# Attention, then two matmul layers, on one core: first loads also from ScalarE's queue, the 1e-9 of the sums on GpSimd, and a new order

## The chip, the cores and the metric

The kernel runs on one core of a Trainium2 chip. The core has five engines that run side by side, each with its own in-order queue of instructions: PE (TensorE, matmuls and transposes), DVE (VectorE), ACT (ScalarE), POOL (GpSimd) and SP (SyncE, which here only issues DMAs). The metric is the device time of one execution in microseconds (us). Three timed runs of the kernel before gave 943.40, 943.42 and 945.23 us; their median is 943.42 us.

## The reference

```
q, k, v: (4 batches, 8 heads, 576 positions, 64)
scores = q @ k.T / 8 + bias            # bias = -slope[head] * distance
scores = where(0 <= row - col < 128, scores, -1e9)
attn = exp(scores - rowmax);  attn = attn / (rowsum(attn) + 1e-9)
x = (attn @ v) laid out as (4*576, 512)
h = x @ w_in                            # 512 -> 2048
g = (a0 + a1 h + a2 h^2 + a3 h^3) / (1 + |b0| |h| + |b1| h^2 + 1e-6)
x = g @ w_out                           # 2048 -> 512
out = (relu(x @ w2_in) ** 2) @ w2_out
```

The weights are 64-bit floats in memory. The kernel makes two fp32r numbers, a high and a low part, of each, and each large matmul is done three times (high by high, high by low, low by high).

## The kernel before, in words

**Attention.** Two heads of one batch are a pair; there are 16 pairs (p0 to p15). Each has five row tiles (units): four of 128 rows and one of the last 64. For a pair, PE transposes q and k (`tr`, L340, and `trr`, L349, for the last 64 rows, which are loaded for all heads of a batch at once into `rem` and `remv`, L316), DVE or ACT copies them from PSUM to `qkT` (L291 or L289), PE makes the scores (`s`, L380 and L369), DVE adds the bias and takes the row extreme (`e`, `st`, L391), ACT takes exp and the row sums (`e`, `sums`, L407), PE transposes the result (`pt`, L442, L437), DVE or ACT copies it (`ptsb`), and PE multiplies it by v (`o`, L468; `or`, L477, L481). The sums of a pair, 9 columns wide, get 1e-9 added (L414) and are inverted (L415), both on DVE, into `rc`. PE transposes `rc` (L420), it is copied to `rt` and sent to memory (`rs`), as is the unnormalised output (`xT` to `xs`).

**Weights.** In the gaps of the attention, the 64 chunks of the weights are loaded (`win1r`, `wout1r`, ...) and split: `w_exp` (L206 on ACT, L209 on POOL or DVE), three steps on DVE (L214, L216, L218), the rounding to the high part (L222, L226) and the subtraction for the low part (L229).

**The two layers.** Blocks of 512 tokens. For the first layer `xs` and `rs` are loaded again (`xr`, and `R`, which spreads one row over 64 partitions, L666), multiplied (L674), and split into `xh` (L226 or L222) and `xl` (L229). The input of the first block comes from batch 0, so the split of its four column groups (c = 0 to 3, from pairs 0 to 3) is done while the attention of later pairs runs. The matmuls are `h` (L694) and `y` (L778).

**What sets the order.** The class `Plan` lists all operations with their engines, costs and predecessors, and orders them one at a time by earliest possible start; ties are broken by a priority in which a table, `BIAS`, adds a number for each kind of operation. The chosen order is then written out: every engine's queue holds its instructions in that order, and an engine whose next instruction waits does nothing else. `warm` (L613) are 22 matmuls on an identity matrix at the start, with no result that is used. All loads are issued by SP before; each DMA uses one of eight completion semaphores in turn, so a DMA waits, at its issue, for the one that stood eight places ahead.

## Time and profile before

| | us |
|---|---|
| median of three runs | 943.42 |
| the profiled execution | 942.65 |
| its span | 940.9 |
| PE busy in the span | 923.6 |
| DVE, ACT, POOL busy | 625.9, 494.9, 324.0 |

The profile is of one execution. Its own time is 1.75 us above its span, and 0.77 us below the median. In the views, busy time is the time in which an engine had at least one instruction running; "idle before" is the engine's idle time just ahead of an instruction, and the arrow names what ended it. "SPq" is a DMA issue by SP.

### The profile page before, as it was taken

The page shows a single profiled execution, that of the slowest core. Times are in us where ns is not written, and L with a number is a line of the kernel's source. Part 1 is how long each engine was busy: PE and PEld are TensorE (multiplying, and loading weights), DVE is VectorE, ACT ScalarE, POOL GpSimd, SP SyncE. Part 2 cuts the span into 40 slices and gives each one's busy share as a digit, 9 for nine tenths or more (in the row PEclk, how much of TensorE's full clock was granted, in tenths as well). Part 3 has the DMA queues.
Part 4 walks back from the last instruction along what each step waited for, and adds up shares of the span by engine and source line. Part 5 has one row for each costly group of instructions (what it writes and reads, how often), then busy time and mean ns, then how long its engine had stood idle before and what let it go on. Part 6 is the DMA issues. An engine that isn't in the chain of part 4 may idle for free.

```text
span 940.9 us, 14096 instructions
## 1 busy us (share of the span) xinstructions
PE 923.6 (98%) x4908; PEld 759.5 (81%) x4908; DVE 625.9 (67%) x1285; ACT 494.9 (53%) x1072; POOL 324.0 (34%) x343
## 2 busy tenths in 40 slices
PE   7999999999999999999999999999999999999998
PEld 5666667888998888888888888888888888888897
DVE  3999998999888886887799987862233223222232
ACT  4988887767767555655666654432222222222222
POOL 5354236867455446444666731030010001000000
PEclk9999999999999999999999999999999999999999
DMA  8999963322402100400142254302000200100010
GB/s 183 236 227 242 241 190 120 115 91 67 132 27 78 35 1 1 125 10 1 37 143 90 68 179 160 133 23 89 1 1 16 74 0 1 68 1 1 1 45 22
DMA packets 102311, 77.01 MB, mean 82 GB/s; under 512 B 64465, under 2 KB 89441, under 8 KB 102241
## 3 DMA queue, kind: packets, MB, share of 16 engines
q1 hardware_dynamic: 102240, 76.12, 28.7%
q8 instruction: 38, 0.62, 0.3%
q14 instruction: 33, 0.26, 0.1%
HBM read 61.87 MB, written 14.23 MB: 81 GB/s over the span
## 4 chain that ended last, share of the span: by engine, by line
PE 87%; DVE 8%; ACT 3%; DMA 1%; issue 1%; SPq 0%; POOL 0%; POOLq 0%; DVEq 0%; ACTq 0%
PE y L778 42%; PE h L694 40%; DVE e L391 3%; ACT e L407 2%; PE tr L340 1%; PE pt L442 1%; DVE wb L218 1%; PE warm L613 1%; DVE qkT L291 1%; DVE wb L216 1%; DMA win1r<-in_moe_w_in_dram 1%; DMA wout1r<-in_moe_w_out_dram 1%; PE o L468 0%; DVE ptsb L291 0%; DVE win1r L214 0%
## 5 line engine op out<-in xcount | busy, mean ns | idle before, releaser
L222 ACT ACTIVATE gh<-h 128x512 fp32r<-128x512 f32 (+1 forms) x160 | 88.7, 555 | 182.4 <-PE y L778 153.4
L229 DVE TENSOR_TENSOR gl<-h,gh 128x512 fp32r<-128x512 f32 (+1 forms) x160 | 101.7, 636 | 122.3 <-ACT gh L222 121.7
L755 DVE SCALAR_TENSOR_TENSOR h<-h,ah 128x512 f32<-128x512 f32 (+1 forms) x80 | 51.6, 645 | 115.0 <-ACT ah L751 114.8
L694 PE MATMUL h<-xh,win1hi 128*128 128x512 f32 (+1 forms) x320 | 118.1, 369 | 1.0 <-DVE gl L229 1.0
L694 PE MATMUL h<-xl,win1hi 128*128 128x512 f32 (+1 forms) x320 | 117.8, 368 | 0.0
L778 PE MATMUL y<-gh,wout1hi 128*128 128x512 f32 (+1 forms) x320 | 117.8, 368 | 0.0
L778 PE MATMUL y<-gl,wout1hi 128*128 128x512 f32 (+1 forms) x320 | 117.7, 368 | 0.0
L694 PE MATMUL h<-xh,win1lo 128*128 128x512 f32 (+1 forms) x320 | 117.7, 368 | 0.0
L778 PE MATMUL y<-gh,wout1lo 128*128 128x512 f32 (+1 forms) x320 | 117.7, 368 | 0.0
L694 PE MATMUL h<-xh,win2lo 128*128 128x512 f32 (+1 forms) x320 | 117.7, 368 | 0.0
L694 PE MATMUL h<-xl,win2hi 128*128 128x512 f32 (+1 forms) x320 | 117.7, 368 | 0.0
L694 PE MATMUL h<-xh,win2hi 128*128 128x512 f32 (+1 forms) x320 | 117.6, 368 | 0.0
L778 PE MATMUL y<-wout2hi,gh 128*128 128x512 f32 x288 | 112.2, 390 | 0.0
L778 PE MATMUL y<-wout2hi,gl 128*128 128x512 f32 x288 | 112.2, 390 | 0.0
L778 PE MATMUL y<-wout2lo,gh 128*128 128x512 f32 x288 | 112.1, 389 | 0.0
L751 ACT ACTIVATE ah<-h 128x512 f32<-128x512 f32 (+1 forms) x80 | 44.4, 554 | 120.9 <-PE h L694 120.4
L719 POOL TENSOR_SCALAR t<-ah,ab_sb 128x512 f32<-128x512 f32 (+1 forms) x80 | 61.7, 772 | 130.6 <-ACT ah L707 114.4
L721 POOL TENSOR_TENSOR t<-t,ah 128x512 f32<-128x512 f32 (+1 forms) x80 | 99.3, 1241 | 5.5
L226 POOL TENSOR_SCALAR xh<-xr 128x512 fp32r<-128x512 f32 (+1 forms) x20 | 13.2, 664 | 249.9 <-PE h L694 248.7
L407 ACT ACTIVATE e<-e,st 128x256 f32<-128x256 f32 (+1 forms) x144 | 67.0, 467 | 8.9 <-DVE st L391 8.7
L694 PEld LDWEIGHTS h<-xh,win1hi 128*128 128x128 f32 x320 | 60.4, 189 | 11.3 <-DVE gl L229 1.3
L694 PEld LDWEIGHTS h<-xh,win2hi 128*128 128x128 f32 x320 | 60.3, 189 | 10.6
(121 smaller groups left out, 1878.7 us busy)
## 6 DMA issues: line engine op xcount, KB each, us to landing
win1r<-in_moe_w_in_dram SPq DMA_DIRECT2D x16, 512.0 KB, 4.8
wout1r<-in_moe_w_out_dram SPq DMA_DIRECT2D x16, 512.0 KB, 3.5
win2r<-in_moe_w_in_dram SPq DMA_DIRECT2D x16, 512.0 KB, 3.8
wout2r<-in_moe_w_out_dram SPq DMA_DIRECT2D x16, 512.0 KB, 3.5
xs<-xT SPq DMA_DIRECT2D x16, 288.0 KB, 4.7
out_dram<-yt SPq DMA_DIRECT2D x18, 256.0 KB, 2.3
vr<-in_v_dram SPq DMA_DIRECT2D x32, 128.0 KB, 3.8
ys<-yt SPq DMA_DIRECT2D x16, 256.0 KB, 2.3
```

What stands on the lines that cost most here:

```text
L216: nc.vector.scalar_tensor_tensor(wb, wb, 3, lw, ALU.logical_shift_left, ALU.bitwise_or)
L222: nc.scalar.activation(dst, src, AF.Copy)
L226: nc.gpsimd.tensor_scalar(dst, src, 1.0, 1.0, ALU.mult, ALU.mult)
L229: (nc.vector if eng == "DVE" else nc.gpsimd).tensor_tensor(dst, a, b, ALU.subtract)
L391: nc.vector.tensor_tensor_reduce(d["e"][:, j, :w], d["s"] if last else d["s"][j], biasl[hp // 2][:, hp % 2, :w] if last else bias8[hp][:, ...
L407: nc.scalar.activation(e, e, AF.Exp, scale=-1.0, bias=s[:, j : j + 1], accum_out=sums[p % 3][:, c : c + 1],)
L694: nc.tensor.matmul(h[:, :n], a[:, c * P : (c + 1) * P], bb[:, :n], start=(m == 0), stop=(m == 3 * NCC - 1),)
L719: nc.gpsimd.tensor_scalar(gt("t", 2, ji, f), ah, ab_sb[:, 1:2], ab_sb[:, 0:1], ALU.mult, ALU.add)
L721: nc.gpsimd.tensor_tensor(tl["t", ji, f], tl["t", ji, f], ah, ALU.mult)
L751: nc.scalar.activation(gt("ah", 2, ji, f), tl["h", ji, f], AF.Relu)
L755: nc.vector.scalar_tensor_tensor(h, h, 0.0, tl["ah", ji, f], ALU.max, ALU.mult)
L778: nc.tensor.matmul(dst, a, bb, start=(f == 0 and m == 0), stop=(f == NF - 1 and m == 2))
```

## The change

Three things. The loads of the first two pairs (`load_qk`, `load_v`, `load_rem`) may be issued by ACT as well as by SP, at the planner's choice. The addition of 1e-9 (`plus`) moves from DVE to POOL, ahead of the reciprocal, which stays on DVE; the exp that writes over the sums three pairs later now waits for `plus` and no longer for the reciprocal. And the table `BIAS` has new numbers, which together with the planner's new entries give a new order on every engine.

```diff
-            if eng == "SP":
+            if self.ops[name][4]:
                 free["DMA"] = max(free.get("DMA", 0.0), end + self.QUEUE) + self.ops[name][4]
...
-BIAS = {'W0': -416.9, 'W1': -833.9, 'W2': 174.9, ...
+BIAS = {'W0': -327.0, 'W1': -452.1, 'W2': 534.2, ...
...
+    def queue(eng):
+        return nc.scalar if eng == "ACT" else nc.sync
...
-            nc.sync.dma_start(
+            queue(eng).dma_start(
                 t[:, t0:t1, j, :], src[b, h0 + j, t0 * P : t1 * P, :].rearrange("(t p) d -> p t d", p=P)
...
+    def plus(p):
+        t = st[p]["rc"] = ap2.tile([P, NSUM], F32, tag="rc", name=f"rc{p}")
+        nc.gpsimd.tensor_scalar(t, sums[p % 3], 1e-9, 1.0, ALU.add, ALU.mult)
+
     def rcp(p):
-        t = st[p]["rc"] = ap2.tile([P, NSUM], F32, tag="rc", name=f"rc{p}")
-        nc.vector.tensor_scalar(t, sums[p % 3], 1e-9, None, ALU.add)
-        nc.vector.reciprocal(t, t)
+        nc.vector.reciprocal(st[p]["rc"], st[p]["rc"])
...
+    def two(p, cost=1.15):
+        return {"SP": cost, "ACT": cost} if p < 2 else {"SP": cost}
...
-                    after=[("ttr", u, j), ("rcp", p - 3)], prio=u,
+                    after=[("ttr", u, j), ("plus", p - 3)], prio=u,
...
-            ("rcp", p), lambda p=p: rcp(p), DVE=0.16,
-            after=[("exp", u, j) for u in range(u0, u0 + NQ) for j in range(2)] + [("rtp", p - 2)], prio=u0 + 4.2, port=True,
-        )
+            ("plus", p), lambda p=p: plus(p), Pool=0.12,
+            after=[("exp", u, j) for u in range(u0, u0 + NQ) for j in range(2)] + [("rtp", p - 2)], prio=u0 + 4.2,
+        )
+        plan.add(("rcp", p), lambda p=p: rcp(p), DVE=0.2, after=[("plus", p)], prio=u0 + 4.2)
```

The new order at three places. The first is the start, on ACT, up to the first exp (`e0`). The number behind a tile's name is its pair (or unit, for `e` and `pt`); the last number only counts buffers. DMAHW0 to DMAHW7 are the eight completion semaphores. Before:

```order
L160 ACT_TABLE_LOAD
L289 ACTIVATE qkT0_214<-tr0_0_0_211 128x256 [waits PE_49]
L289 ACTIVATE qkT0_214<-tr1_0_0_221 128x256 [waits PE_49]
L289 ACTIVATE qkT0_214<-tr0_0_2_231 128x256 [waits PE_49]
L289 ACTIVATE qkT0_214<-tr1_0_2_238 128x256 [waits PE_49]
L407 ACTIVATE e0_259,sums0_154<-e0_259,st0_258 128x128 [waits DVE_49]
```

And now, on the same engine, up to the same exp:

```order
L160 ACT_TABLE_LOAD
L311 DMA qr0_167<-in_q_dram 128x2x64 x2
L311 DMA kr0_164<-in_k_dram 128x2x64
L311 DMA kr0_164<-in_k_dram 128x2x64 [waits DMAHW0_49]
L289 ACTIVATE qkT0_204<-tr0_0_0_201 128x256 [waits PE_49]
L289 ACTIVATE qkT0_204<-tr1_0_0_213 128x256 [waits PE_49]
L319 DMA rem_0_229<-in_q_dram 64x8x64 [waits DMAHW3_49]
L319 DMA rem_0_229<-in_k_dram 64x8x64 [waits DMAHW4_49]
L319 DMA remv0_150<-in_v_dram 64x8x64 [waits DMAHW7_49]
L410 ACTIVATE e0_262,sums0_154<-e0_262,st0_261 128x128 [waits DVE_49]
```

Four loads of pair 0 now stand right behind the table load, two of the four copies have gone to DVE, and the three loads of the last 64 rows of batch 0 stand ahead of the first exp. SP issues kr0, vr0, the second half of qr0, vr1, qr1, win1r of chunk 0 and kr1 in this time; the semaphore that remv0 waits for, DMAHW7, is the one that the first load of kr1 uses just before.

On PE the start reads so before:

```order
L613 MATMUL warm_167<-ident_107 128x128 x16
L340 MATMUL tr0_0_0_211<-ident_107,qr0_182 128x128 x2
L613 MATMUL warm_167<-ident_107 128x128 x3
L340 MATMUL tr1_0_0_221<-ident_107,kr0_162 128x128 x2
L613 MATMUL warm_167<-ident_107 128x128 x3
L340 MATMUL tr0_0_2_231<-ident_107,qr0_182 128x128 x2
L340 MATMUL tr1_0_2_238<-ident_107,kr0_162 128x128 x2
L380 MATMUL s0_0_0_246<-qkT0_214 128x128
```

And now:

```order
L623 MATMUL warm_170<-ident_107 128x128 x11
L343 MATMUL tr0_0_0_201<-ident_107,qr0_167 128x128 x2
L623 MATMUL warm_170<-ident_107 128x128 x2
L343 MATMUL tr1_0_0_213<-ident_107,kr0_164 128x128 x2
L623 MATMUL warm_170<-ident_107 128x128 x9
L343 MATMUL tr0_0_2_233<-ident_107,qr0_167 128x128 x2
L343 MATMUL tr1_0_2_242<-ident_107,kr0_164 128x128 x2
L383 MATMUL s0_0_0_246<-qkT0_204 128x128
```

The first transposes stand five `warm` matmuls earlier; the number of `warm` matmuls ahead of the first scores is 22 as before.

The second place is POOL around the input of the first layer's column group 1 (`xr0_1`). Before:

```order
L209 TENSOR_SCALAR wb6_870<-win1r_6_746 128x512
L229 TENSOR_TENSOR win1lo_6_928<-wb6_870,win1hi_6_927 128x512
L674 TENSOR_TENSOR xr0_1_820<-xr0_1_820,R0_1_822 128x512
L226 TENSOR_SCALAR xh0_1_992<-xr0_1_820 128x512
L229 TENSOR_TENSOR xl0_1_1004<-xr0_1_820,xh0_1_992 128x512
L229 TENSOR_TENSOR win1lo_7_1056<-wb7_969,win1hi_7_1055 128x512
```

And now:

```order
L209 TENSOR_SCALAR wb5_827<-win1r_5_681 128x512
L684 TENSOR_TENSOR xr0_1_737<-xr0_1_737,R0_1_739 128x512
L226 TENSOR_SCALAR xh0_1_868<-xr0_1_737 128x512
L229 TENSOR_TENSOR xl0_1_886<-xr0_1_737,xh0_1_868 128x512
L417 TENSOR_SCALAR rc4_913<-sums1_155 128x9
L226 TENSOR_SCALAR win1hi_5_916<-wb5_827 128x512
```

The addition of 1e-9 for pair 4 stands behind the three operations on column group 1; that of pair 3 stands in the same way behind group 0, and that of pair 5 behind group 2.

The third place is PE at the change from attention to the first layer. Before:

```order
L442 MATMUL pt77_2342<-ident_107,e77_2298 128x128 x4
L369 MATMUL s15_2_2351<-qkT15_2202 64x192 x2
L468 MATMUL o15_2360<-ptsb15_2326,vr15_2138 64x256 x4
L442 MATMUL pt78_2373<-ident_107,e78_2304 128x128 x4
L437 MATMUL pt79_2381<-ident_107,e79_2366 128x128 x2
L694 MATMUL h0_0_2388<-xh0_0_804,win1hi_0_317 128x512
...
L468 MATMUL o15_2360<-ptsb15_2326,vr15_2138 64x256 x2
L420 MATMUL or15_2502<-ident_107,rc15_2384 9x128
```

And now:

```order
L372 MATMUL s15_2_2358<-qkT15_2223 64x192 x2
L447 MATMUL pt77_2366<-ident_107,e77_2315 128x128 x4
L473 MATMUL o15_2382<-ptsb15_2356,vr15_2156 64x256 x4
L704 MATMUL h0_0_2390<-xh0_0_719,win1hi_0_348 128x512
...
L425 MATMUL or15_2497<-ident_107,rc15_2388 9x128
L447 MATMUL pt78_2499<-ident_107,e78_2321 128x128 x4
L442 MATMUL pt79_2509<-ident_107,e79_2373 128x128 x2
L473 MATMUL o15_2382<-ptsb15_2356,vr15_2156 64x256 x2
```

Left out are the 48 matmuls of h0_0 to h0_3 in both. The transposes of the last two units (pt78, pt79) moved behind them, and behind h0_4 a whole step more (h0_5) now stands ahead of the first y.

## Rows read from the trace of the kernel before

**Rows 1.** Busy time by stage: stretch, length, busy us of each engine (instructions), clock, DMA.

```profile
0.00:10.40 10.40, 8.58 (x52) 8.26 (x52) 0.06 (x1) 2.43 (x4) 8.57 (x27) 1.00 0.62 149
10.40:30.00 19.60, 15.67 (x123) 10.03 (x123) 14.80 (x58) 14.25 (x50) 4.46 (x5) 1.00 0.97 214
30.00:92.00 62.00, 58.02 (x516) 40.56 (x513) 58.34 (x219) 52.30 (x184) 29.06 (x29) 1.00 0.97 238
92.00:146.00 54.00, 51.45 (x461) 36.16 (x460) 49.64 (x189) 45.91 (x160) 18.71 (x20) 1.00 0.80 204
146.00:160.00 14.00, 13.41 (x72) 10.47 (x71) 11.96 (x21) 11.26 (x20) 9.95 (x10) 1.00 0.33 113
160.00:936.00 776.00, 775.63 (x3692) 653.69 (x3691) 491.08 (x803) 367.55 (x656) 253.21 (x253) 1.00 0.18 56
```

**Rows 2.** Waits of PE: what, for whom: us in total, times, longest.

```profile
PE tr L340 <- DVE qkT L291: 2.3, 8, 0.6
PE s L369 <- DVE qkT L291: 1.6, 3, 1.0
```

**Rows 3.** Timeline of the start: start, length, instruction [idle before, what ended it].

```profile
0.72 1.28 ACT L160 ACT_TABLE_LOAD   x1 [0.72 <-PEq L929]
...
1.35 6.26 PE L613 MATMUL warm<-ident 128*128 128x128 f32 x32 [1.35 <-POOL ident masks.py:199]
...
4.87 0.98 SPq L308 DMA_DIRECT2D qr<-in_q_dram  x2
...
7.44 0.38 PE L340 MATMUL tr<-ident,qr 128*128 128x128 f32 x2
...
10.12 0.44 PE L340 MATMUL tr<-ident,kr 128*128 128x128 f32 x2 [0.47 <-ACT qkT L289]
...
11.90 0.40 ACT L407 ACTIVATE e<-e,st 128x128 f32<-128x128 f32 x1 [0.93 <-DVE st L391]
...
12.12 0.65 POOL L209 TENSOR_SCALAR wb<-win1r 128x512 f32<-128x512 f32 x1 [1.87 <-DMA win1r<-in_moe_w_in_dram]
...
12.51 0.64 SPq L316 DMA_DIRECT2D remv<-in_v_dram  x1
```

**Rows 4.** Groups by line and shape, attention: count | busy, mean ns | idle before.

```profile
L289 ACT ACTIVATE ptsb<-pt 128x512 f32<-128x512 f32 x29 | 16.7, 587 | 2.4 <-PE pt L442 2.2
L291 DVE COPY ptsb<-pt 128x512 f32<-128x512 f32 x19 | 13.0, 684 | 0.6 <-PE pt L442 0.6
L226 POOL TENSOR_SCALAR win1hi<-wb 128x512 fp32r<-128x512 f32 x9 | 5.6, 617 | 31.9 <-DVE wb L218 27.1 <-DVE rc L414 4.9
L280 POOL TENSOR_SCALAR bias<-rel 128x256 f32<-128x256 f32 x8 | 3.2, 402 | 0.5
L414 DVE TENSOR_SCALAR rc<-sums 128x9 f32<-128x9 f32 x16 | 5.4, 336 | 0.9 <-ACT e L407 0.9
```

**Rows 5.** All instructions of line L414: ns min/median/max, first and last start.

```profile
L414 DVE TENSOR_SCALAR rc<-sums x16: 149/168/1194, 20.4 to 145.2; 128x9 f32<-128x9 f32 x16
```

**Rows 6.** Timeline: pair 1's output copied, pair 4's sums, and column group 1 on POOL.

```profile
39.03 0.22 ACT L289 ACTIVATE xT<-or 128x64 f32<-128x64 f32 x1
...
45.88 1.27 POOL L674 TENSOR_TENSOR xr<-xr,R 128x512 f32<-128x512 f32 x1
45.99 1.19 DVE L414 TENSOR_SCALAR rc<-sums 128x9 f32<-128x9 f32 x1
...
54.44 0.16 DVE L414 TENSOR_SCALAR rc<-sums 128x9 f32<-128x9 f32 x1
...
58.11 1.28 POOL L674 TENSOR_TENSOR xr<-xr,R 128x512 f32<-128x512 f32 x1
...
60.23 1.28 POOL L229 TENSOR_TENSOR xl<-xr,xh 128x512 fp32r<-128x512 f32 x1
```

**Rows 7.** DMA issues: count, KB each, median us from issue to landing.

```profile
xs<-xT SPq DMA_DIRECT2D x16, 288.0 KB, 4.7
...
R<-rs SPq DMA_DIRECT2D x12, 128.0 KB, 6.9
```

**Rows 8.** Timeline of PE where the first layer begins.

```profile
144.39 1.08 PE L468 MATMUL o<-ptsb,vr 128*64 128x256 f32 x8 [0.72 <-ACT e L407]
...
159.16 0.50 PE L694 MATMUL h<-xh,win1hi 128*128 128x512 f32 x1 [0.59 <-DVE gl L229]
```

More of the change, by code (lines that the diff above doesn't have):

```diff
@@ L97, in run @@
             fn(eng) if len(engs) > 1 else fn()
-BIAS = {'W0': -416.9, 'W1': -833.9, 'W2': 174.9, 'W3': -153.9, 'attn_end': 896.0, 'bias': -332.0, 'exp': 84.0, 'g1': 159.6, 'g2': 163.5, 'gh': 2.9, 'gl': -268.1, 'ldk': 57.5, 'ldk0': -338.4, 'ldq': 99.3, 'ldq0': 331.9, 'ldr': 377.8, 'ldv': 105.8, 'ptc': -247.7, 'ptp': 268.5, 'pv': 64.8, 'r_abs': 33.0, 'r_g1': 63.2, 'r_g2': -144.0, 'r_g3': -694.3, 'r_p1': 486.9, 'r_p2': 266.4, 'r_r1': 109.8, 'r_r2': 206.0, 'r_t1': -202.8, 'r_t2': -379.6, 'r_u': -91.6, 'rcp': -171.9, 'rout': 202.1, 'rtc': -511.3, 'rtp': -541.3, 's': -127.0, 's_g': -91.3, 's_relu': -222.2, 'scl': -214.7, 'scp': 712.6, 'trk': 99.1, 'trk0': 101.2, 'trk0c': -324.6, 'trkc': 290.0, 'trq': -28.9, 'trq0': -378.1, 'trq0c': -90.4, 'trqc': 356.2, 'trr': 192.3, 'trrc': -666.1, 'ttr': -675.7, 'w0': 396.4, 'w1': 108.0, 'w2': 400.3, 'w3': -491.9, 'w4': -326.2, 'w5': -103.3, 'warm': 442.5, 'wl': -405.2, 'x': 124.7, 'xh': -413.4, 'xl': -200.5, 'xld': -1.2, 'xn': -207.3, 'xo': 145.8, 'xr': 36.3, 'yc': -225.0, 'yo': -531.9}
+BIAS = {'W0': -327.0, 'W1': -452.1, 'W2': 534.2, 'W3': -655.2, 'attn_end': -522.7, 'bias': -400.9, 'exp': -80.2, 'g1': 132.6, 'g2': 136.0, 'gh': -479.3, 'gl': -60.7, 'ldk': 191.3, 'ldk0': -235.8, 'ldq': -274.9, 'ldq0': 305.3, 'ldr': -520.4, 'ldv': 519.8, 'plus': -817.6, 'ptc': 1025.2, 'ptp': 745.7, 'pv': 441.5, 'r_abs': -183.2, 'r_g1': 814.4, 'r_g2': -428.3, 'r_g3': 749.6, 'r_p1': 99.0, 'r_p2': 785.2, 'r_r1': 255.9, 'r_r2': 200.3, 'r_t1': -328.0, 'r_t2': 199.0, 'r_u': 336.1, 'rcp': 173.4, 'rout': -258.7, 'rtc': -79.5, 'rtp': -594.7, 's': -385.4, 's_g': 169.0, 's_relu': -109.2, 'scl': 481.9, 'scp': 140.1, 'trk': 228.7, 'trk0': -279.6, 'trk0c': -452.8, 'trkc': -123.7, 'trq': 449.7, 'trq0': -229.8, 'trq0c': 234.2, 'trqc': -140.5, 'trr': 158.5, 'trrc': -357.9, 'ttr': -775.4, 'w0': 38.2, 'w1': 1068.6, 'w2': 822.1, 'w3': -182.5, 'w4': 303.1, 'w5': -256.3, 'warm': 98.4, 'wl': 15.1, 'x': -148.6, 'xh': 414.4, 'xl': -391.2, 'xld': -437.4, 'xn': -480.1, 'xo': 517.8, 'xr': 114.1, 'yc': 45.9, 'yo': 8.8}
 WEIGHT = 0.0000
@@ L299, in parts, with load_qk @@
         return [("0", 0, 2), ("", 2, NQ - 1)] if p == 0 else [("", 0, NQ - 1)]
-    def load_qk(p, nme, src, t0, t1):
+    def queue(eng):
+        return nc.scalar if eng == "ACT" else nc.sync
+    def load_qk(eng, p, nme, src, t0, t1):
         b, hp = pairs[p]
@@ L307, in load_qk, with load_rem @@
         for j in range(2):
-            nc.sync.dma_start(
+            queue(eng).dma_start(
                 t[:, t0:t1, j, :], src[b, h0 + j, t0 * P : t1 * P, :].rearrange("(t p) d -> p t d", p=P)
             )
-    def load_rem(b, srcs=(q, k, v)):
+    def load_rem(eng, b, srcs=(q, k, v)):
         rem[b] = araw.tile([P, H, D], F32, tag="rem", name=f"rem_{b}"), remv[b % 2]
         for dst, src in zip((rem[b][0][:LAST], rem[b][0][P - LAST :], rem[b][1][P - LAST :]), srcs):
-            nc.sync.dma_start(dst, src[b, :, MAIN:, :].rearrange("h p d -> p h d"))
+            queue(eng).dma_start(dst, src[b, :, MAIN:, :].rearrange("h p d -> p h d"))
     rem = {}
@@ L321, in tile_window_attention_moe_moe, with load_v @@
         nc.gpsimd.memset(t[: P - LAST], 0.0)
-    def load_v(p):
+    def load_v(eng, p):
         b, hp = pairs[p]
@@ L327, in load_v @@
         for j in range(2):
-            nc.sync.dma_start(
+            queue(eng).dma_start(
                 t[:, :, j, :], v[b, h0 + j, :MAIN, :].rearrange("(t p) d -> p t d", p=P)
@@ L512, in tile_window_attention_moe_moe @@
                     (f"ld{nme}{part}", p),
-                    lambda p=p, nme=nme, src=src, t0=t0, t1=t1: load_qk(p, nme, src, t0, t1),
-                    SP=1.15, move=1.46 * w,
+                    lambda eng="SP", p=p, nme=nme, src=src, t0=t0, t1=t1: load_qk(eng, p, nme, src, t0, t1),
+                    **two(p), move=1.46 * w,
                     after=[("trkc", p - 2), ("ld" + nme, p - 1)] + ([] if part else [("ldk0", p)]),
@@ L518, in tile_window_attention_moe_moe @@
         plan.add(
-            ("ldv", p), lambda p=p: load_v(p), SP=1.15, move=1.46,
+            ("ldv", p), lambda eng="SP", p=p: load_v(eng, p), **two(p), move=1.46,
             after=[("pv", u0 - VB * NQ + NQ - 1), ("ldv", p - 1)], prio=u0 - 6,
@@ L523, in tile_window_attention_moe_moe @@
             plan.add(
-                ("ldr", b), lambda b=b: load_rem(b), SP=1.9, move=2.2,
+                ("ldr", b), lambda eng="SP", b=b: load_rem(eng, b), **two(p, 1.9), move=2.2,
                 after=[("pv", u0 - NPAIR * NQ - 1), ("trr", p - NPAIR - 1), ("ldr", b - 1)] + [("ldk", 0)][:p == 0],
```

## The prediction

> **What bounds the kernel now.** I read the busy time by stage first [rows 1], because the kernel is two kinds of work with different limits. From 160 us to 936 us PE is busy 775.63 of 776 us: the two layers are PE's, the change leaves their matmuls and, after the first steps, PE's order of them as they were, so this stretch can neither give nor be given anything but the 0.37 us that it idles. All that can be won stands before 160 us, and it is PE's idle time there, stretch less busy: 1.82 us up to 10.4 us, 3.93 us up to 30 us, 3.98 us up to 92 us, 2.55 us up to 146 us and 0.59 us up to 160 us, 12.87 us in all. Of it, 1.35 us is the wait for the identity matrix [rows 3], which stays. So the most that any order of these instructions can give back is about 11.5 us, 1.2% of the time, and a loss has to show as idle time of PE that is not there now. In the middle of the attention (30 to 146 us) PE is busy 94%, DVE 93% and ACT 85%: PE leads, and DVE is close enough to hold it up. The waits of PE say the same: the longest are for DVE's copies of qkT, 2.3 and 1.6 us [rows 2].
>
> **The loads of the start: 0.** The transposes of q do not wait for a load now: the `warm` matmuls run without a gap from 1.35 us to 7.61 us, and the first transpose follows at 7.44 us with no idle time before it [rows 3]. A load that lands earlier therefore only lets the first transposes change places with `warm` matmuls, and all 22 of these still stand ahead of the scores. That is the work that hides the gain. What was idle there, 0.47 us ahead of the last transpose of k [rows 3], waits for a copy and stays.
>
> A rule of the Trainium skill speaks against this part as well (DMA: Bandwidth & Descriptors, "Issuing engines are not separate DMA queues"): DMAs that several engines issue run on the same 16 DMA engines and interleave, and a second issuing engine only saves sequencer time. The trace agrees as far as it goes, for the DMA engines are 0.97 busy from 10.4 to 30 us [rows 1]; by the rule this term is 0 too, and loads behind the first ones land no earlier.
>
> **The last 64 rows' loads on ACT: +0.6 us.** The first exp now stands behind the issue of remv0, and that issue waits until the first load of kr1 has landed. Ahead of that landing are 1920 KB, by the shapes of the tiles at 4 bytes a number: 512 of q and k of pair 0, 512 of v of two pairs, 256 of q of pair 1, 512 of win1r, 128 of itself. In the kernel before, win1r was complete at 12.12 us, when 1536 KB were in [rows 3]. At the rates of the two first stretches, 149 and 214 GB/s [rows 1], counted from about 1.2 us, 1920 KB take until 14.1 or 10.2 us. I take 12.5 us, near the landing of win1r. With 0.64 us for the issue of remv [rows 3], ACT is free at 13.15 us; the first exp started at 11.90 us, so it comes 1.2 us late (bounds 0 and 2.8). Behind the exp are the transposes of the first units on PE, and nothing else covers them. But ACT has less to do right after: the copies of pt0 and pt1 went to DVE, which has done its eight `e` rows by then, and I let that give back half. +0.6 us (0 to +2.8).
>
> **The 1e-9 on POOL: -1.9 us.** DVE loses 16 instructions of 336 ns, 5.4 us [rows 4]; their median is 168 ns and their longest 1194 ns [rows 5], and the long one runs while POOL is in an operation of 1.27 us [rows 6], so half of the cost was a wait for POOL. No row shows this operation on POOL. By the two TENSOR_SCALAR rows, 402 ns for 256 columns and 617 ns for 512 [rows 4], an estimate for 9 columns is 0.19 us, nothing beside POOL's idle time. The new step does not only remove work: the reciprocal now follows a signal from ACT to POOL and one from POOL to DVE. Of the 5.4 us, what PE sees is at most what it idles for DVE; the two waits in [rows 2] are 3.9 us. I take half of that, -1.9 us, between 0 (PE was waiting for something else each time) and -5.4 us (all of DVE's time on the path).
>
> Which of the two engines waits is what the skill has a rule for (SBUF — State Buffer, "Who interferes with whom"): for certain pairs of instructions DVE and GpSimd share a port as an exclusive lock, and the one that comes second is blocked until the first is done. The trace shows such a hold in the 1194 ns of L414. By the rule the hold does not vanish with the move but passes to POOL's instruction, behind which the reciprocal now waits; the term would be 0, and the sum 1.9 us higher, still within the forecast's own case.
>
> **POOL's queue: +1.0 us.** POOL is in order, so `plus` of pair 4 starts only when xr, xh and xl of column group 1 are done. These need R, which needs rs and xs of pair 1. Pair 1's output is copied at 39.25 us [rows 6]; xs lands 4.7 us after its issue and R 6.9 us [rows 7], with some 0.5 us between: R lands near 51.4 us if SP issues both at once, and the new order has fewer loads ahead of them. From the start of xr to the end of xl it was 58.11 to 61.51, 3.4 us [rows 6]. So `plus` starts at 54.8 us and ends at 55.0 us, and L414 ran at 54.44 us: DVE would stand still for 0.6 us ahead of the reciprocal, with the next pair's `e` rows queued behind it and ACT and PE behind those. Pairs 3 and 5 have the same arrangement. Three times 0.6 us, of which work that PE still has queued hides about half: +1.0 us. If R comes as late as it did, `plus` would end at 61.7 us, 7.3 us late, at one place; if it comes 1 us earlier the term is 0.
>
> **The change to the first layer: -1.3 us.** PE idled 0.72 us at 144.39 us for an exp, and 0.59 us at 159.16 us for the first step's gl [rows 8]. Now pt78 and pt79 stand behind four steps of h, so that the late exps are waited for under other work, and h0_5 fills the time for gl. The matmuls stay the same in number. If both waits only move, the term is 0.
>
> **Copies that change engines: 0.** Up to the last `e` row, DVE takes 14 more copies of pt (11 of them of 512 columns, 684 ns each against ACT's 587 [rows 4]) and gives ACT 15 copies of q and k. With the steps of one more weight chunk this makes about 1 us more for DVE over the attention, beside the 8.0 us that it idles between 30 and 146 us [rows 1]. I take 0, within 1 us.
>
> **The sum.** +0.6 - 1.9 + 1.0 - 1.3 = -1.6 us on the profiled execution's 942.65 us: 941.05 us. That execution is 0.77 us under the median of the runs, so on the median's level 943.42 - 1.6 = 941.8 us.
>
> **Rivals.** A measurement of this kernel can tell about 0.2% (1.9 us) from no change: faster is below 941.5 us, slower above 945.3 us.
> *The forecast, a small gain that is lost in the measurement:* 941.8 us, own range 941.5 to 945.3 us. For it: the start is covered, and terms of both signs nearly cancel.
> *A clear gain.* PE's waits for DVE were the main thing that held the pairs up, and the relief of DVE and the copies given to ACT take them all: -3.9 us in place of -1.9, the first exp is not late (0 in place of +0.6), POOL's queue costs 0.5 us less. Sum -3.9 - 1.3 + 0.5 = -4.7 us, 938.7 us. For it: the pool of 10.5 us of idle time between 10.4 and 146 us, largest at the start, where the new order does least besides attention. Against it: the average pair in the middle leaves PE under 0.5 us idle, so a gain must come a bit from every pair.
> *Slower: the reciprocal waits for `plus` behind the first layer's input.* One mechanism, on POOL, at pairs 3, 4 and 5. Price: 2.6 us at each place if R lands 2 us later than I worked out and nothing is hidden, 7.8 us in place of +1.0. Sum +0.6 - 1.9 + 7.8 - 1.3 = +5.2 us, 948.6 us. It decides from about 1.5 us of lateness at each place, where the sum passes +1.9 us. For it: R took 6.9 us to land in the median, and `plus` has no other way past. Against it: SP has fewer issues ahead of xr now, and DVE is not ahead of PE everywhere.
>
> **How the numbers follow.** Forecast 0.42, clear gain 0.40, slower 0.18. The range has 938.8 us at the low end, where the clear gain's middle lies, and 945.6 us at the high end, a little into the slower case; outside are perhaps 1 in 10 on either side.
>
> **What would show it.** The loads: the first scores on PE again near 10.5 us. The issue of remv: idle time of ACT ahead of the first exp, ended by a DMA or by its own queue, and that exp between 12 and 14.7 us. The 1e-9: L417 near 0.2 us on POOL, DVE's idle time ahead of L420 small, PE's waits for qkT below 3.9 us. POOL's queue: idle time of DVE ahead of L420 for pairs 3 to 5, ended by POOL rc, of about 0.6 us; over 1.5 us each and the slower case holds. The change to the first layer: no gap at the first h and none at h0_4. The forecast is wrong if PE's idle time before 160 us has changed by more than 2 us, or if any idle time appears after it.

## The result, and the profile after

The changed kernel takes 951.19 us (median of 6 runs, 948.64 to 952.07), the kernel before 943.41 us beside it (942.34 to 945.23): ratio 1.0076, 95% interval 1.006 to 1.0093. It is slower, by 7.8 us between the medians and by 7.2 us (0.76%) as the ratio gives it, which sets runs side by side; the shares below go by ratios. The prediction, 941.8 us, had the wrong sign, and the time lies outside its range. The profiled execution's span is 950.0 us against 940.9 us, 9.1 us more.

Lines of the changed file are up to 10 higher than in the one before: the exp is L410, the transpose of the exponentials L447, the reciprocal L420, the first layer's product L704. First the busy time by stage, in the columns of [rows 1].

```profile
0.00:10.40 10.40, 8.51 (x54) 7.92 (x54) 0.48 (x2) 2.05 (x3) 8.57 (x27) 1.00 0.71 157
10.40:30.00 19.60, 14.62 (x102) 9.62 (x102) 13.60 (x54) 12.05 (x44) 1.08 (x3) 0.91 1.03 198
30.00:92.00 62.00, 58.62 (x514) 39.95 (x514) 56.54 (x204) 49.10 (x176) 34.58 (x39) 1.00 0.97 233
92.00:146.00 54.00, 51.91 (x460) 35.82 (x458) 50.90 (x192) 46.88 (x164) 18.35 (x23) 1.00 0.86 217
146.00:160.00 14.00, 12.54 (x71) 9.73 (x68) 11.03 (x23) 8.96 (x21) 8.49 (x9) 1.00 0.42 134
160.00:936.00 776.00, 772.80 (x3676) 649.78 (x3675) 489.94 (x800) 364.65 (x655) 255.38 (x258) 1.00 0.18 55
```

Two stretches stand out. From 10.4 to 30 us PE idles 4.98 us (3.93 before) and its clock is 0.91 (1.00 before). Behind 160 us, where the old kernel's PE idled 0.37 us, it idles 3.20 us. But over the whole span PE's idle time has grown by only 3.9 us, and the span by 9.1: the other 5.2 us are busy time (923.6 us before, 928.8 now). The next view, in the same columns, has two stretches of 5 us with a mean clock of 0.66; by an estimate from that clock (5 times 0.34) they lost up to 1.7 us each, 3.4 us together. Where the rest of the busy time comes from is open.

```profile
10.40:15.00 4.60, 1.75 (x17) 1.24 (x16) 3.00 (x17) 0.28 (x1) 0.00 (x0) 1.00 1.29 217
15.00:20.00 5.00, 4.19 (x20) 2.73 (x21) 2.72 (x6) 3.82 (x17) 0.00 (x0) 0.66 1.00 143
160.00:165.00 5.00, 2.46 (x16) 1.51 (x14) 5.00 (x10) 4.83 (x10) 3.17 (x4) 1.00 0.00 1
165.00:170.00 5.00, 4.95 (x15) 3.92 (x16) 5.00 (x9) 2.29 (x5) 1.33 (x2) 0.66 0.55 161
```

**The start.** The timeline of ScalarE from 8 to 15 us (start, length, instruction, idle time before and what ended it; ACTq is its queue issuing DMAs) answers to the start in [rows 3]:

```profile
8.46 0.68 ACTq L319 DMA_DIRECT2D rem<-in_q_dram  x1
9.18 0.65 ACTq L319 DMA_DIRECT2D rem<-in_k_dram  x1
14.07 0.60 ACTq L319 DMA_DIRECT2D remv<-in_v_dram  x1
14.72 0.40 ACT L410 ACTIVATE e<-e,st 128x128 f32<-128x128 f32 x1 [7.05 <-DMA rem<-in_k_dram]
```

The first two issues were out at 9.83 us. The third stood until 14.07 us for an earlier load's completion, and the first exp with it: 14.72 us in place of 11.90. PE, in the same view:

```profile
10.36 1.79 PE L383 MATMUL s<-qkT 64*128 64x128 f32 x16
15.27 0.33 PE L447 MATMUL pt<-ident,e 128*128 128x128 f32 x1 [3.12 <-ACT e L410]
16.14 1.12 PE L447 MATMUL pt<-ident,e 128*128 128x128 f32 x4 [0.55 <-ACT e L410]
```

The scores are as early as before; then PE waits 3.12 us, and from about 16 to 19 us the same rows come at 0.21 us each in place of 0.11: that is the clock of 0.66 above.

**The junction.** PE where the first layer has begun, and VectorE beside it, in the same view. This answers to [rows 8]:

```profile
160.88 0.27 PE L425 MATMUL or<-ident,rc 128*9 128x128 f32 x1
160.99 0.60 PE L447 MATMUL pt<-ident,e 128*128 128x128 f32 x4
...
162.69 0.65 PE L473 MATMUL o<-ptsb,vr 128*64 128x256 f32 x4 [0.89 <-ACT ptsb L289]
165.05 0.50 PE L704 MATMUL h<-xh,win1hi 128*128 128x512 f32 x1 [1.71 <-DVE gl L229]
```

```profile
160.60 0.75 DVE L757 SCALAR_TENSOR_TENSOR h<-u,ca_sb,h 128x512 f32<-128x512 f32 x1
...
162.51 0.68 DVE L216 SCALAR_TENSOR_TENSOR wb<-wb,wout1r 128x512 int32<-128x512 int32 x1
163.12 0.69 DVE L757 SCALAR_TENSOR_TENSOR h<-t,h 128x512 f32<-128x512 f32 x1
163.71 0.68 DVE L218 SCALAR_TENSOR_TENSOR wb<-wout1r,wb 128x512 int32<-128x512 int32 x1
164.31 0.68 DVE L229 TENSOR_TENSOR gl<-h,gh 128x512 fp32r<-128x512 f32 x1
```

In the kernel before, the same two steps of VectorE were:

```profile
156.56 0.76 DVE L747 SCALAR_TENSOR_TENSOR h<-u,ca_sb,h 128x512 f32<-128x512 f32 x1
...
158.42 0.69 DVE L229 TENSOR_TENSOR gl<-h,gh 128x512 fp32r<-128x512 f32 x1
```

The first chunk's gl followed the step that makes its input by 1.86 us, with two instructions between them; now it follows by 3.71 us, with five between. VectorE has no idle time there in either kernel, so what differs is its order, and not how busy it is.

The fifth block of the first layer starts at 165.05 us in place of 159.16, 5.89 us late; 3.83 us of that are there when the layer begins (149.87 us against 146.04 in the two timelines), the rest is these two waits against the 0.59 us of before. The other 3.2 us of the 9.1 come behind this row: about 1.5 at the low clock to 169 us, the last pair's remaining products, which stood ahead before, and two later waits for gl of 0.3 us each.

**The 1e-9.** The groups of the two instructions:

```profile
L417 POOL TENSOR_SCALAR rc<-sums 128x9 f32<-128x9 f32 x16 | 5.8, 362 | 18.3 <-ACT e L410 17.3
...
L420 DVE RECIPROCAL rc<-rc 128x9 f32<-128x9 f32 x16 | 3.4, 210 | 2.4 <-POOL rc L417 1.8
```

DVE waited for POOL twice, 1.8 us together; the longer wait, 1.45 us at 49.0 us, is at pair 3, where the prediction put it.

### The profile page after: what moved, and what is told of

Its sections match the earlier page's. It is cut to its first block, busy times and chain, and to the rows that moved or that the text cites. A ratio compares the mean times of both kernels' runs of the same rounds, so it can differ in the third digit from the quotient of the medians.

```text
span 950.0 us, 14127 instructions
## 1 busy us (share of the span) xinstructions
PE 928.8 (98%) x4908; PEld 760.9 (80%) x4908; DVE 624.6 (66%) x1275; ACT 486.8 (51%) x1067; POOL 326.4 (34%) x358
## 4 chain that ended last, share of the span: by engine, by line
PE 86%; DVE 6%; DMA 3%; ACT 3%; issue 1%; POOL 1%; SPq 0%; ACTq 0%; DVEq 0%; POOLq 0%
PE y L788 40%; PE h L704 40%; ACT e L410 1%; PE pt L447 1%; DVE e L394 1%; PE o L473 1%; DMA win1r<-in_moe_w_in_dram 1%; PE s L383 1%; PE tr L343 1%; DVE h L757 1%; DMA R<-rs 1%; DMA kr<-in_k_dram 1%; DVE ptsb L291 1%; DVE t L757 1%; DMA xs<-xT 0%
## 5 line engine op out<-in xcount | busy, mean ns | idle before, releaser
L704 PE MATMUL h<-xh,win1hi 128*128 128x512 f32 (+1 forms) x320 | 118.6, 371 | 2.0 <-DVE gl L229 2.0
L704 PE MATMUL h<-xh,win1lo 128*128 128x512 f32 (+1 forms) x320 | 118.4, 370 | 0.0
L704 PE MATMUL h<-xl,win1hi 128*128 128x512 f32 (+1 forms) x320 | 118.4, 370 | 0.0
L704 PE MATMUL h<-xh,win2lo 128*128 128x512 f32 (+1 forms) x320 | 117.7, 368 | 0.0
L704 PE MATMUL h<-xl,win2hi 128*128 128x512 f32 (+1 forms) x320 | 117.7, 368 | 0.0
L704 PE MATMUL h<-xh,win2hi 128*128 128x512 f32 (+1 forms) x320 | 117.6, 368 | 0.0
L410 ACT ACTIVATE e<-e,st 128x256 f32<-128x256 f32 (+1 forms) x144 | 67.1, 467 | 15.5 <-DVE st L394 8.3
L704 PEld LDWEIGHTS h<-xh,win1hi 128*128 128x128 f32 x320 | 60.7, 190 | 13.2 <-DVE gl L229 2.7
L704 PEld LDWEIGHTS h<-xh,win1lo 128*128 128x128 f32 x320 | 60.7, 190 | 10.2
```

What stands on the lines that cost most here:

```text
L410: nc.scalar.activation(e, e, AF.Exp, scale=-1.0, bias=s[:, j : j + 1], accum_out=sums[p % 3][:, c : c + 1],)
L704: nc.tensor.matmul(h[:, :n], a[:, c * P : (c + 1) * P], bb[:, :n], start=(m == 0), stop=(m == 3 * NCC - 1),)
```

## The experiments

Ratios are against the kernel before on the same chip, with the 95% interval. By the profile the theory was: two losses, the first in the loads of the last 64 rows on ScalarE, the second in the new order behind the attention. In the expectations, theory A.

### Do the loads of the last rows cost the start?

```diff
-            queue(eng).dma_start(dst, src[b, :, MAIN:, :].rearrange("h p d -> p h d"))
+            nc.sync.dma_start(dst, src[b, :, MAIN:, :].rearrange("h p d -> p h d"))
```

> The changed kernel in its own order, with only the loads of the last 64 rows of the first batch (rem, remv) issued from SyncE again; they stand there behind qr1 and ahead of the first weight chunk. Theory A (the third of these loads held ScalarE until 14.67 us and so the first exponential; that is one of two losses): the first exponential starts near 12 us, TensorE's wait of 3.1 us at 12.15 is under 0.7 us, no stretch between 15 and 20 us is at the low clock, the first matmul of the first layer starts near 147 us (149.87 in the changed kernel, 146.04 in the kernel before), and the time is about 948.5 us, 2 to 3.5 under the changed kernel. Rival B (the attention has slack and takes the late start back; the order of the later work is the whole loss): the first exponential is earlier but the time stays within 1 us of 951.2. Rival C (the 1e-9 on GpSimd is the loss): no change either.

Measured: 947.12 us, 1.0042 (1.0028 to 1.0056). PE, in the timeline:

```profile
12.83 0.33 PE L447 MATMUL pt<-ident,e 128*128 128x128 f32 x1 [0.17 <-ACT e L410]
...
161.35 0.50 PE L704 MATMUL h<-xh,win1hi 128*128 128x512 f32 x1 [1.74 <-DVE gl L229]
```

The first wait is 0.17 us, the clock is 1.00 from 15 to 20 us, and the first layer begins at 146.15 us, as before. The second wait is untouched, but no low clock follows it in this execution. So by the ratios the start is worth 1.0076 less 1.0042, 0.34% or 3.2 us (some 1 to 5 us by the two intervals); in the trace it is the whole delay of 3.83 us with which the first layer began. Part of the 3.2 us may be the clock at the junction. The reverse: the kernel before with the same three loads on ScalarE.

```diff
-            nc.sync.dma_start(dst, src[b, :, MAIN:, :].rearrange("h p d -> p h d"))
+            (nc.sync if b else nc.scalar).dma_start(dst, src[b, :, MAIN:, :].rearrange("h p d -> p h d"))
```

> The kernel before in its own order, with only the loads of the last 64 rows of the first batch issued from ScalarE, ahead of its first exponential. Theory A: the first exponential starts 1 to 3 us later than 11.90, TensorE waits as long ahead of the first transposes of the exponentials, and the kernel is slower by 1.5 to 4 us: 945 to 947.5. If the loss lay in the new order and not in the place of these loads: within 0.7 us of the kernel before.

Measured: 949.64 us, 1.006 (1.0047 to 1.0072), more than expected. ScalarE and PE in its timeline:

```profile
12.79 0.71 ACTq L316 DMA_DIRECT2D rem<-in_q_dram  x1
15.43 0.61 ACTq L316 DMA_DIRECT2D rem<-in_k_dram  x1
17.11 0.60 ACTq L316 DMA_DIRECT2D remv<-in_v_dram  x1
17.76 0.40 ACT L407 ACTIVATE e<-e,st 128x128 f32<-128x128 f32 x1 [6.53 <-DMA rem<-in_q_dram]
...
18.31 0.48 PE L442 MATMUL pt<-ident,e 128*128 128x128 f32 x1 [5.77 <-ACT e L407]
```

Here all three issues had to wait, and PE stood 5.77 us. Is it the wait of an issue alone? The changed kernel, with only the third load on SyncE:

```diff
-            queue(eng).dma_start(dst, src[b, :, MAIN:, :].rearrange("h p d -> p h d"))
+            (nc.sync if src is v else queue(eng)).dma_start(dst, src[b, :, MAIN:, :].rearrange("h p d -> p h d"))
```

> The changed kernel with one of the three loads of the last 64 rows (remv, the third) issued from SyncE and the other two still from ScalarE. If the loss at the start is the wait of that one issue for an earlier load's completion (it stood at 14.07 to 14.67 us, the other two were out at 9.84): first exponential near 12 us, ratio 1.0035 to 1.005 as with all three on SyncE. If each issue on ScalarE costs by itself, or the second load now meets such a wait: first exponential after 13.5 us and ratio 1.006 or more.

Measured: 951.9 us, 1.0086 (1.0072 to 1.01). Neither expectation held. ScalarE's and PE's timeline:

```profile
9.97 0.65 ACTq L319 DMA_DIRECT2D rem<-in_k_dram  x1
11.09 0.40 ACT L410 ACTIVATE e<-e,st 128x128 f32<-128x128 f32 x1 [4.11 <-DVE st L394]
...
17.59 0.30 PE L352 MATMUL trr<-ident,rem 128*128 128x128 f32 x1 [3.15 <-DMA rem<-in_k_dram]
```

The first exp was not held, at 11.09 us. But PE then waited 3.15 us for the rows themselves: those of the keys, issued at 9.97 us, were there 7.6 us later. With all three on SyncE that issue was at 7.77 us, the last one ended at 9.07 us, and this transpose did not wait. So the theory was half right: the hold of the exp is real, but without it the same rows, issued 2.2 us later from ScalarE, hold PE as long at its next step. Whether the later issue, the queue or the loads ahead of them made them late, the runs do not tell apart.

### Is part of it the clock?

Fillers (transposes of the identity) in PE's wait, in the changed kernel; first 28, which was a mistake in size, since each leaves two rows of 0.11 us, then 14.

```diff
     def pt_pe(u):
+        for _ in range(14 if u == 0 else 0):
+            nc.tensor.matmul(tl["warm"][:, :P], ident, ident, start=True, stop=True)
```

> The changed kernel with 28 more filler products of 128 columns on TensorE, put right ahead of the first transposes of the exponentials, where it waits 3.1 us; 28 at 0.11 us are 3.1 us. The wait itself stays; only its idleness goes. Theory A (of the loss at the start some 1.5 us are the low clock from 16 to 19 us that follows the idle time, but the pair behind has slack of about as much): no stretch at the low clock before 150 us, the first matmul of the first layer 0.5 to 1.5 us earlier than 149.87, time 949.7 to 950.7. Rival E (the clock costs nothing here, the late exponential is all): first layer within 0.3 us of 149.87, and 951.2. If the fillers end after the exponential is there, they cost up to 0.5 us themselves.

> The changed kernel with 14 filler products in TensorE's wait at the start, in place of the 28 that took twice the time of the wait (each leaves two rows of 0.11 us). The exponentials stay as late as in the changed kernel. Theory A with the clock: no stretch at the low clock before 100 us, first matmul of the first layer 0.8 to 2 us earlier than 149.87, time 1 to 2 us under the changed kernel (ratio to before 1.0055 to 1.0065). Rival E (the clock costs nothing there): within 0.3 us of it.

With 28 the fillers took 6.52 us and held the transposes until 17.79 us: 953.31 us, 1.0098 (1.0083 to 1.0114), which only shows that they cost. With 14: 949.64 us, 1.0055 (1.0039 to 1.007). The windows of the run with 14, in the columns of [rows 1]:

```profile
15.00:20.00 5.00, 4.83 (x40) 3.23 (x40) 3.81 (x7) 3.85 (x15) 0.00 (x0) 1.00 1.20 167
...
163.00:167.00 4.00, 3.66 (x9) 2.95 (x10) 4.00 (x8) 2.27 (x5) 1.60 (x2) 0.57 0.56 173
```

The clock stays at 1.00 at the start, PE starts the transposes 0.31 us later than in the changed kernel (15.58 us), and the first layer yet begins 1.72 us earlier, at 148.15 us. In that execution the exp came at 13.77 us, 0.95 us earlier, so not all of it is the clock; by the ratios the low clock is up to 2.0 us of the 3.2, with intervals that overlap. At the junction, which it leaves alone, the clock was low again.

### Is the second loss one late instruction?

In the run with all three loads on SyncE, the first chunk's last steps were put ahead of other work on VectorE and ScalarE, and then, in a run of its own, the end of the attention ahead of the first layer; the order is otherwise kept. Each pair of the list puts its first step right ahead of its second. A third run has both lists, without the move of the copy ptc 78 ahead of rtc 15.

```diff
-WEIGHT = 0.0000
+WEIGHT, MOVES = 0.0000, [(('r_g3', 0, 0), ('r_p1', 0, 2)), (('gh', 0, 0), ('rtc', 15)), (('ptc', 78), ('rtc', 15)), (('gl', 0, 0), ('r_g1', 0, 1))]
```

> The changed kernel with the loads of the last 64 rows of the first batch on SyncE, and four steps of the first layer's first chunk put earlier, without any other change: its last activation step on VectorE ahead of the next chunk's first product, its rounding (gh) on ScalarE ahead of the copy of the reciprocals and of the next absolute value, the copy of the second-last transposed scores right behind it, and its low part (gl) ahead of the weight bits that stood before it. Theory A (second loss: gl of the first chunk stands behind some 5 instructions of other work on VectorE and 3 on ScalarE in the new order, and TensorE waits 1.7 us for it): the wait ahead of the fifth block of the first layer shrinks from 1.74 to under 0.5 us, and the time is 1.0 to 2.0 us under the run with only the loads moved (947.1), near 945.5. Rival D (what follows is as tight, and the time gained is waited for at the next chunk): the wait moves on by some 12 to 15 us in the program and the time stays at 947.

Measured: 948.71 us, 1.0045 (1.0032 to 1.0058): no gain. In PE's timeline the wait ahead of the fifth block is gone, and stands at the next one, as rival D said:

```profile
164.48 0.50 PE L704 MATMUL h<-xh,win1hi 128*128 128x512 f32 x1 [2.70 <-DVE gl L229]
```

```diff
-WEIGHT = 0.0000
+WEIGHT, MOVES = 0.0000, [(('ptp', 78), ('g1', 0, 0)), (('ptp', 79), ('g1', 0, 0)), (('ptc', 78), ('g1', 0, 0)), (('ptc', 79), ('g1', 0, 0)), (('pv', 79), ('g1', 0, 4)), (('xo', 15), ('gh', 0, 1)), (('xr', 15), ('r_p2', 0, 3)), (('g2', 0, 0), ('g1', 0, 5))]
```

> The changed kernel with the loads of the last 64 rows on SyncE, and with the transposes of the last pair's last two blocks and their copies put ahead of the first layer, their products, the two copies of its output ahead of the fifth block's end, and the first second-layer product ahead of the sixth block; gl of the first chunk stays where it was. Theory H (the junction's loss is not one late instruction: the new order leaves the end of the attention behind four blocks of the first layer, so the second product cannot start and TensorE needs the next gl, which VectorE, busy throughout, has not made yet): TensorE starts the first layer 0.3 to 0.8 us later than in the run with the loads moved (146.15), waits up to 1.7 us for the first gl, and then no more; 0.5 to 1.5 us under that run (ratio to the kernel before 1.003). If the order of the attention's end did not matter: ratio 1.004 as before.

> As the run with the attention's end first, and with the first chunk's last step, gh and gl earlier, as in the run with four steps moved. Theory H: both together give back the junction of the kernel before: the wait ahead of the fifth block under 0.6 us, none over 0.6 us ahead of the sixth, time within 1 us of the kernel before (ratio 0.9995 to 1.001), some 3 us under the run with only the loads moved. Rival: VectorE has too much work there in the new order whatever stands first, and 2 us or more remain (ratio over 1.002).

The end of the attention first: 951.03 us, 1.007 (1.0055 to 1.0084), worse, with 2.62 us ahead of the fifth block and the low clock behind it. Both together: 949.74 us, 1.0053 (1.0037 to 1.0068). The first expectation failed; of the second, theory H holds for the wait and its rival for the time. PE's timeline of the run with both:

```profile
165.79 0.50 PE L704 MATMUL h<-xh,win1hi 128*128 128x512 f32 x1 [0.28 <-DVE gl L229]
...
221.10 0.50 PE L704 MATMUL h<-xh,win1hi 128*128 128x512 f32 x1 [0.45 <-DVE gl L229]
...
248.96 0.39 PE L704 MATMUL h<-xh,win1hi 128*128 128x256 f32 x1 [0.66 <-DVE gl L229]
```

The wait at the junction is nearly gone, but new ones stand 60 to 90 us later, and from 170 to 300 us PE idles 2.62 us, against 0.37 us in the kernel before. One reading is that all that follows was ordered for another junction, so that only the order as a whole can be good. The last two runs take it whole: the loads on SyncE, the order of one kernel up to the first product of the first layer and of the other behind it; `moved()` gives names and engines from such a list.

```diff
-        for _, _, name, eng in sorted(order):
+        for name, eng in moved():
```

> The changed kernel with the loads of the last 64 rows on SyncE, in its own order up to the first product of the first layer, and everything that is left by then in the order (and on the engines) of the kernel before. Theory I (the second loss, 3.3 us up to 170 us and 0.7 us after it in the run with the loads moved, is the new order from the end of the attention on, and nothing ahead of it): the two last transposes go ahead of the first layer as before, TensorE waits under 0.9 us for the first gl and not again, and the time is within 1 us of the kernel before, ratio 0.9995 to 1.001. Rival J (what the new order did ahead of the first layer, which engine did which weight step and how far the weights are, makes VectorE late whatever follows): 2 us or more remain, ratio over 1.002.

> The reverse: loads of the last rows on SyncE, 1e-9 on GpSimd, the order of the kernel before up to the first product of the first layer, and everything that is left in the order and on the engines of the changed kernel. Theory I: the loss comes with the later order, ratio 1.003 to 1.005. Rival J: within 1 us of the kernel before.

The new order up to the first layer and the old one behind it: 943.02 us, 0.9996 (0.9987 to 1.0005). The second loss is gone, 1.0042 to 0.9996, 0.46% or 4.3 us (some 3 to 6 us by the two intervals), and with it all of the slowness. PE's timeline and waits:

```profile
160.46 0.50 PE L704 MATMUL h<-xh,win1hi 128*128 128x512 f32 x1 [0.30 <-DVE gl L229]
```

```profile
PE h L704 <- DVE gl L229: 0.7, 2, 0.4
```

The reverse is 954.3 us, 1.0111 (1.0097 to 1.0125): slower as expected, but by more than the second loss, with one wait of 9.45 us for gl ahead of the fifth block. Its trace says where, against the run with the new order throughout (all three loads on SyncE in both), in PE's and VectorE's timelines:

```profile
151.21 0.69 DVE L216 SCALAR_TENSOR_TENSOR wb<-wb,wout1r 128x512 int32<-128x512 int32 x1 [2.47 <-POOL wb L209]
157.27 0.68 DVE L737 TENSOR_TENSOR u<-u,h 128x512 f32<-128x512 f32 x1
167.32 0.79 PE L704 MATMUL h<-xh,win1hi 128*128 128x512 f32 x1 [9.45 <-DVE gl L229]
```

```profile
150.50 0.69 DVE L737 TENSOR_TENSOR u<-u,h 128x512 f32<-128x512 f32 x1 [0.50 <-ACT u L721]
```

Behind the old attention VectorE first splits three chunks of weights, where it splits two behind the new one, and waits 2.47 us for GpSimd on the way; the layer's first step on it runs at 157.27 us in place of 150.50 (the second fence). So the new tail loses behind either part. That the size hangs on how far the weights are by then is a reading of these rows, which no run puts to the test.

### The 1e-9, and the loads of the start

The addition on GpSimd, alone in the kernel before; and back on VectorE in the changed kernel:

```diff
-        nc.vector.tensor_scalar(t, sums[p % 3], 1e-9, None, ALU.add)
+        nc.gpsimd.tensor_scalar(t, sums[p % 3], 1e-9, 1.0, ALU.add, ALU.mult)
```

> The kernel before in its own order with the addition of 1e-9 alone moved to GpSimd, nothing else changed. Theory A: 0 to 1.9 us faster than before, 941.5 to 943.4 us. Rival C: slower by 2 us or more, with TensorE waiting ahead of the transposes of the reciprocals (L420).

> The changed kernel in its own order, with the addition of 1e-9 on VectorE again, right ahead of its reciprocal. Theory A: the addition comes back to VectorE for some 0.17 to 0.34 us a pair, 0 to 1.9 us in all beyond what idle time takes: 951 to 953 us. Rival C (the step on GpSimd makes the reciprocal late, and this is the loss): 944 to 948 us.

Measured: 943.06 us, 0.9991 (0.9982 to 1.0), and 949.7 us, 1.0068 (1.0054 to 1.0082), which overlaps with the changed kernel. By the first the move is worth some 0.8 us (0 to 1.7), by the second nothing that shows. In the first the waits of VectorE have a row:

```profile
DVE rc L415 <- POOL rc L414: 5.4, 7, 1.5
```

VectorE stood 5.4 us for it, as long as the instruction had taken there [rows 4], and the time did not rise. PE's waits for the copies on VectorE, which the prediction wanted halved, have these rows there:

```profile
PE tr L340 <- DVE qkT L291: 2.5, 6, 1.0
PE s L369 <- DVE qkT L291: 1.6, 3, 1.0
```

They are as long as before, 2.3 and 1.6 us [rows 2], with the addition gone from VectorE.

For the loads, the changed kernel with all on SyncE; the kernel before with the first half of the first queries and the second of the keys on ScalarE; without 9 of the fillers at the start (1e-9 on GpSimd); and with all of these:

```diff
-            nc.sync.dma_start(
+            (nc.scalar if p == 0 and (nme == "q") == (t0 == 0) else nc.sync).dma_start(
-        for _ in range(WARM if k == 0 else 1):
+        for _ in range(WARM if k == 0 else k < 8 or k in (13, 14)):
```

> The changed kernel in its own order, with every load issued from SyncE: what is left of the change is the new order and the 1e-9 on GpSimd. Theory A: the start is that of the run with the last rows alone on SyncE, within 0.7 us (first exponential near 12.2 us; the first scores near 10.5 us, since the first query load now stands ahead of the first value load); time 948 to 949.5 us, so that some 5 us over the kernel before stay with the new order. If issuing from two engines at the start is a gain by itself, this run is slower than the run with the last rows alone on SyncE by 0.5 to 1.5 us. Rivals B and C: 951 us.

> The kernel before with the first half of the first pair's queries and the second half of its keys issued from ScalarE at the start, and nothing else. Theory F (all fillers must run before the scores, so the earlier landing is not seen): ratio 0.9995 to 1.0005, first scores within 0.7 us of 10.49. If issuing from two engines gains by itself: 0.9985 or less.

> The kernel before with the addition of 1e-9 on GpSimd and without the 9 filler products, all loads on SyncE. If the fewer fillers alone made the faster kernel (ratio 0.9974): 0.997 to 0.998, with the first scores as early. If it needs the loads from ScalarE as well (first scores held by the landing of the first pair's loads): ratio 0.9985 to 0.9995.

> The kernel before in its own order, with the three parts of its change that need not cost: of the first pair's loads the first half of the queries and the second half of the keys issued from ScalarE at the start (no loads of the last rows), the addition of 1e-9 on GpSimd, and 9 of the filler products at the start left out, so that the transposes may follow the loads. Theory F: the first scores start near 8.5 to 9 us in place of 10.49; if the attention passes the gain on, 1 to 2 us faster than before (ratio 0.998 to 0.999). Rival (as in the run without fillers in the new order, the gain of the start is eaten before the attention ends, since VectorE and ScalarE, over 90% busy, set the pace): ratio 0.9985 to 1.0005, first layer within 0.5 us of 146.04.

All on SyncE: 947.88 us, 1.0042 (1.0029 to 1.0054), so the second queue gave the changed kernel nothing. In the kernel before, two queues alone: 1.0001 (0.9991 to 1.0011); fewer fillers alone: 0.9999 (0.9988 to 1.0009); all together: 941.66 us, 0.9974 (0.9963 to 0.9985), faster than both kernels. Its PE at the start, in the timeline:

```profile
7.61 0.44 PE L340 MATMUL tr<-ident,qr 128*128 128x128 f32 x2 [0.47 <-ACT qkT L289]
...
8.89 1.79 PE L380 MATMUL s<-qkT 64*128 64x128 f32 x16
```

By the ratios each edit hides the other's gain. The traces of single executions do not say how. The first scores started at 10.49 us before, at 9.55 with two queues alone, at 9.15 with fewer fillers alone and at 8.89 with all together, so in these executions either edit alone brought them forward. The moment at which the fillers go from 0.21 to 0.11 us each differs between executions as well. With all together the first layer begins only 0.25 us earlier than before (145.79 for 146.04 us), so where the rest of the 0.26% comes from is open. Does the new attention order pass such a start on?

> As the run with the four steps moved (loads of the last rows on SyncE), and without the last 9 filler products at the start, which stand ahead of the transposes of the first pair's second part. Theory F (the earlier landing of the first loads is hidden by a fixed number of fillers on TensorE, so that issuing from two engines could not show): the first scores start at 8.3 to 9.2 us in place of 10.4 to 10.9, and the time falls by 1 to 2 us against the run without this edit. Rival G (TensorE then waits for the loads or for the copies of the transposes, or runs at the low clock longer): within 0.5 us.

> The run with the attention in the changed kernel's order, everything behind it in the order of the kernel before and the loads of the last rows on SyncE (ratio 0.9996), now also without the last 9 fillers at the start. If the attention passes the earlier start on, as in the kernel before with two queues and fewer fillers (0.9974): 0.997 to 0.9985. If in this order the start's gain is eaten by 100 us, as in the earlier run without fillers: 0.999 to 1.0005.

Without the 9 fillers, the run with the first four steps moved took 948.13 us, 1.0042 (1.0025 to 1.0058), though its scores began at 8.38 us, 1.6 us earlier than with the fillers. That is the time of rival G; the first layer begins at 145.63 us there and at 145.50 with the fillers, so the gain is gone before the first layer; by what stays open. With the old tail and fewer fillers it was 942.3 us, 0.998 (0.997 to 0.999), also faster than both kernels; with the fillers it was 0.9996 (0.9987 to 1.0005), and the two intervals overlap.

## Why the prediction was wrong

- **The loads of the start, 0:** right by the times (two queues alone, 1.0001), as the prediction had it, with the fillers to cover them. That they do is not shown: in the trace of that run the first scores start at 9.55 us in place of 10.49.
- **The last 64 rows' loads on ScalarE, +0.6:** the mechanism was named, the size was not: 3.2 us. The hold reached the upper bound of its first step (14.72 us). Three things were missed: that nothing gives it back (the exp is 2.82 us late, and the first layer 3.83 us); that PE's clock falls after such a wait; and that the rows are needed soon after the first exps, so that their landing matters as well as the issue of the third.
- **The 1e-9 on GpSimd, -1.9:** failed. The term took half of what PE waits for VectorE's copies. With the move alone these waits stay (2.5 and 1.6 us for 2.3 and 1.6), so the addition did not cause them; in the changed kernel they shrink to 0.7 and 0.5 us, and the time shows no gain there either. The move gave some 0.8 us (0 to 1.7).
- **GpSimd's queue, +1.0:** the wait came, at one of three places (1.45 us), and costs nothing that the runs can tell.
- **The change to the first layer, -1.3:** failed, and in sign: +4.3 us. It counted the two old waits as covered, and held that the sixth block (h0_5) fills the time for gl. The wait for gl stands ahead of the fifth block (h0_4), though, 1.71 us now in place of 0.59, and the sixth comes behind it in PE's order, so it can't fill it. The sixth needs the next chunk's gl itself, and the twelve matmuls of the second product that stood between the two blocks before (162.04 to 164.76 us) stand there no longer. And gl itself comes later behind its input, 3.71 us in place of 1.86. The step read which waits go and not what stands there next. With the old order from the first layer on, the time goes from 1.0042 to 0.9996.
- **Copies that change engines, 0:** right as far as the runs tell: with loads and tail as before the new attention order gives 0.9996.

The prediction also held that a loss has to show as idle time of PE. That failed in part: of the 9.1 us of span, 5.2 are busy time of PE, up to 3.4 of them at the low clock.

By the ratios the loss is 3.2 us for the loads and 4.3 us for the tail, less 0.4 us by which the run without both was faster than the kernel before. These are steps of one chain, 1.0076 to 1.0042 to 0.9996 to 1, so they add up by construction, and that they do is no check. The rival "slower" named another mechanism, which was there and was not the loss. The rule of the Trainium skill on the port that VectorE and GpSimd share (SBUF — State Buffer, "Who interferes with whom"), by which one of the two is blocked until the other is done, was the rival that gave 0 for the 1e-9. The measured 0.9991 (0.9982 to 1.0) has 0 at its edge, and no row tells whether by this mechanism.

## What to carry to other kernels

A load that is issued from a computing engine's queue costs that engine the wait for the load's own turn: put none there whose turn comes when the engine has work, and ask when its data is needed. A part of an order that was found for the whole was worth nothing here: a late instruction moved forward moved the wait, and only the exchange of a whole stage's order took the loss away. When a transfer is hidden behind fixed filler work, neither edit alone may show a gain; try both together.
